# k's maxima by GpSimd in six batches, and the two halves of k'v taken apart, in a kernel that interleaves attention with a feed-forward layer

## The chip, the cores and the metric

The kernel runs on one core of one Trainium2 chip. The metric is the time of one execution on the device in microseconds (us), as the median of several runs. Beside the runs there is one profiled execution, whose trace holds every instruction of every engine. The engines are named as the profile names them: PE (TensorE matmul), PEld (TensorE weight load), DVE (VectorE), ACT (ScalarE), POOL (GpSimd) and SP (SyncE, which here issues nearly all DMAs).

## What is computed

The inputs are q, k and v of 8 batches, 8 heads, 576 rows and 64 columns, and two weights of 512 x 2048 and 2048 x 512. First comes a linear attention, then a feed-forward layer over its 4608 x 512 output:

```python
q_s = exp(q - q.max(-1));  q_s = q_s / (q_s.sum(-1) + 1e-9)      # over the 64 columns
k_s = exp(k - k.max(2));   k_s = k_s / (k_s.sum(2) + 1e-9)       # over the 576 rows
kv  = einsum('bhsd,bhse->bhde', k_s, v)
x   = einsum('bhsd,bhde->bhse', q_s, kv)      # then to rows (batch, row) and columns (head, d)
h   = x @ w_in
out = (h * erf(softplus(h))) @ w_out
```

The maximum of k runs over the rows of a batch, and these lie over the 128 partitions. So it is a maximum over partitions, for each of the 8 x 64 = 512 columns.

## The kernel before

**Feed-forward.** The 4608 rows of x are cut into four pairs of batches, each pair into three blocks of 384 rows, and each block meets four groups of 512 hidden columns: 48 items, n = 0 to 47. For item n the first product runs in four steps `mm1(n, 0..3)`. It is a 2 x 2 block product by seven half-size products: seven calls of `prod` (line 990) of 12 f16 matmuls each, of which `mm1` 0, 1, 2 and 3 hold 2, 2, 1 and 2. DVE and ACT take the results out of three PSUM banks, X, Y and Z. ACT computes softplus and erf, DVE multiplies and splits the result into two f16 halves (`gmul`, `ghi`, `glo`), and `mm2(n, 0..2)` does the second product, 12 f16 matmuls of 512 columns a step (line 1125). The loop from line 1224 writes for each n: `mm1(n, 0)`, `mm2(n-2, 0)`, `mm1(n, 1)`, `mm2(n-2, 1)`, `mm1(n, 2)`, `mm2(n-2, 2)`, `mm1(n, 3)`.

**Attention.** Batch 0 stands in an order written out by hand (line 33), and so does the interleaving of batch 1. Batches 2 to 7 are steps of the generator `attention16` (line 649). At each `yield` it returns a share, a number that stands for how much of the pair's attention this step is. After each `mm2` step the function `pace` (line 1207) takes further steps until the sum of shares has reached a goal that grows with n, a fixed amount for a pair of batches. So there are three slots in each n, here written n.0, n.1 and n.2, at which attention work is put among the feed-forward work. A yield of 0 ends the slot.

A batch goes like this before the change. `k_max` (DVE) takes the maximum of each partition over its rows. `k_max_T` (line 504) transposes the 128 x 512 result with four TensorE transposes into a PSUM bank kT, and a DVE reduce (line 512) gives the column maxima km. `k_max_rows` (line 517) spreads them over all partitions with four more transposes into a PSUM bank kB. DVE subtracts kB from k in three pieces (lines 662 and 667; kt is the batch's 64 last rows) and each row's maximum from q (`q_sub`). ACT takes the exponentials. Then for each of the two halves of four heads: `kv_mm` multiplies k' by v, where a column of ones beside v gives the sums, and `kv_norm` divides; `q_norm` divides q; `q_halves` splits q into two f16 parts (ACT line 640, DVE line 641) and transposes them with a DMA from SP (line 643). After both halves `kv_max` and `kv_split` scale kv into f16 halves in `kvbd` (lines 595, 596), with one more transpose for the scale (`x_bk`, line 125). Last come the products x = q' kv: `xt` for the last rows of the pair, in odd batches only, and four blocks x0 to x3 (line 632).

**What sets the order.** The code's order is not the engines' order. A planner of the framework orders each engine's instructions by when it reckons them ready, so that DVE often works ahead of the code. `tc.issue_after(i)` queues an instruction behind i on its engine. ACT's exponentials, softplus and erf are chained in this way, in the order of the code (`act`, line 339). Each engine runs its queue in order, and so does each DMA queue. v has one buffer for both halves of the heads (`vbuf`), so `load_half(v, "v", b, 1)` waits for the first half's `kv_mm`, and the second half's `kv_mm` waits for that load.

The tiles that the steps below touch: the small SBUF tag `qT` of two buffers (k's maxima, kvf), and two PSUM banks of the tag `bk` (kT, kB, k'v, x_bk, xt, x).

Of the kernel before, what the change touches and what calls it, by code (L numbers as in the profile page):

```python
# [1 line left out]

# [7 lines left out]
F32 = mybir.dt.float32  # L10
# [35 lines left out]
OUTS = [0, 1, 2, 3]  # L46

SHARES = [2.51, 0, 0.16, 0.09, 1.58, 2.43, 1.12, 0.26, 0.29, 0.04, 0.78, 1.12, 0.16]
SHARES16 = [2.51, 0, 0.16, 0.09, 1.58, 2.43, 1.3, 2.43, 1.3, 0.26, 0.3, 0.78, 0.3]
LEAD = 2.0  # L50

EXPMASK = 0x7F800000
# [5 lines left out]
def attn_moe_kernel(  # L58
# [9 lines left out]
    nc = tc.nc  # L68
# [270 lines left out]
    def act(out_, in_, func, chain=True, **kw):  # L339

        with ExitStack() as es:
            if chain and last[0] is not None:
                es.enter_context(tc.issue_after(last[0]))
            i = nc.scalar.activation(out_, in_, func, **kw)  # L344
        if chain:
            last[0] = i.ins
        return i
# [144 lines left out]
    def k_max(b, ks, kt):  # L492

        kmax = at.tile([P, H, D], F32, tag="qT", name=f"kmax_{b}")
        k2 = at.tile([P, 2, 4, D], F32, tag="qT", name=f"k2_{b}")
        for hf in range(2):
            nc.vector.tensor_tensor(k2, ks[hf][:, 0:2], ks[hf][:, 2:4], op=ALU.max)
            nc.vector.tensor_tensor(
                kmax[:, hf * 4:hf * 4 + 4, :], k2[:, 0], k2[:, 1], op=ALU.max
            )  # L500
        nc.vector.tensor_tensor(kmax[kt[1]], kmax[kt[1]], kt[0], op=ALU.max)
        return kmax

    def k_max_T(b, kmax):
        bk = bank(f"kT_{b}")
        km2 = hd(kmax)
        for c in range(NC4):
            nc.tensor.transpose(
                bk[:, c * P:(c + 1) * P], km2[:, c * P:(c + 1) * P], ident
            )  # L510
        km = at.tile([P, NC4], F32, tag="km", bufs=1, name=f"km_{b}")
        nc.vector.tensor_reduce(
            km, bk.rearrange("p (c s) -> p c s", c=NC4), axis=AX.X, op=ALU.max
        )
        return km

    def k_max_rows(b, km):

        bk = bank(f"kB_{b}")
        for c in range(NC4):  # L520
            nc.tensor.transpose(
                bk[:, c * P:(c + 1) * P], km[:, c:c + 1].to_broadcast([P, P]), ident
            )
        return bk.rearrange("p (h d) -> p h d", h=H)

    W = D + 1

    def kv_mm(b, hf):
# [104 lines left out]
                out_, kvbd[b % 2][:, wl, c, :], qT[:, ql], start=(i == 0), stop=(i == 2)  # L633
            )

    def q_halves(src, place, name):

        n = src.shape[1]
        st_ = place.bitcast(F16).rearrange("p (i n) -> p i n", i=2)
        nc.scalar.copy(st_[:, 0], src)  # L640
        nc.vector.tensor_tensor(st_[:, 1], src, st_[:, 0], op=ALU.subtract)
        qT = src.bitcast(F16).rearrange("p (a s) -> p a s", s=P)
        nc.sync.dma_start_transpose(qT, place.bitcast(F16))
        return qT.rearrange("p (i a) s -> p i a s", i=2)

    def flat3(t):
        return t.rearrange("p a b c -> p (a b c)")

    def attention16(b):
        d, j, p = bat[b], b % 2, b // 2  # L650
        even = bat[b - j]
        tl = slice(j * TAIL, (j + 1) * TAIL)
        ks, qs, kt = d["k"], d["q"], even["kt"][tl]
        sh = iter(SHARES16)
        kmax = k_max(b, ks, (kt, tl))
        yield next(sh)
        km = k_max_T(b, kmax)
        q_sub(rows(qs[0]), 16, f"q_{b}_0")
        yield next(sh)
        kb = k_max_rows(b, km)  # L660
        for hf in range(2):
            nc.vector.tensor_tensor(
                ks[hf], ks[hf],
                kb[:, None, hf * 4:hf * 4 + 4, :].to_broadcast([P, TM, 4, D]),
                op=ALU.subtract,
            )
        nc.vector.tensor_tensor(kt, kt, kb[tl], op=ALU.subtract)
        yield next(sh)
        q_sub(rows(qs[1]), 16, f"q_{b}_1")
        if j == 1:  # L670
            q_sub(even["qt"], H, f"qt_{p}")
        yield next(sh)
        for t in (*ks, kt, qs[0], qs[1], *([even["qt"]] if j == 1 else [])):
            act(t, t, AF.Exp, chain=b > 1)
        yield next(sh)
        qT = {}
        for hf in range(2):
            kv_norm(b, hf, kv_mm(b, hf))
            if hf == 0:
                d["v"].append(load_half(v, "v", b, 1))  # L680
            q_norm(rows(qs[hf]), 16, f"q_{b}_{hf}", b)
            yield next(sh)
            qT[hf] = q_halves(flat3(qs[hf]), flat3(ks[hf]), f"{b}_{hf}")
            yield next(sh)
        if j == 1:
            q_norm(even["qt"], H, f"qt_{p}", b)
            qT[2] = q_halves(hd(even["qt"]), hd(even["kt"]), f"{p}_t")
        if b + 1 < B:
            load_kv(b + 1)
        mx = kv_max(b)  # L690
        yield next(sh)
        kv_split(b, mx)
        yield next(sh)
        for i in ((3 * p + 1, 3 * p + 2) if j else (3 * p, 3 * p + 1)):
            while not x_free(i):
                yield 0
        w = next(sh)
        if j == 1:
            bk = bank(f"xt_{p}")
            x = xblock(p * NBK + 1)  # L700
            bk3 = bk.rearrange("p (c s) -> p c s", c=NC4)
            for a in range(2):
                for c in range(NC4):
                    cs = slice(a * TAIL, (a + 1) * TAIL)
                    x_mm(2 * p + a, c, bk3[:, c, cs], qT[2][:, :, c, cs])
            x_put(bk3, x[:, :, SM - T:SM - T + P], None)
            if b + 1 < B:
                bat[b + 1]["qt"] = load_tail(q, "qt", p + 1)
            yield w
        w = next(sh)  # L710
        for c in range(NC4):
            hf, c2 = divmod(c, 2)
            bk = bank(f"x_{b}_{c}")
            q4 = qT[hf].rearrange("p i (t c) s -> p i t c s", c=2)[:, :, :, c2]
            x_mm(b, c, bk.rearrange("p (t s) -> p t s", t=TM), q4)
            x_split(b, c, bk)
            if c2 == 1 and b + 1 < B:
                load_q(b + 1, hf)
            if c == NC4 - 1:
                d["xdone"] = True  # L720
            yield w

    def x_split(b, c, bk, part=None):
        for blk, off, o, w in xcols(b, 0 if b % 2 == 0 else SM + 2 * TAIL, SM)[part or slice(9)]:
# [250 lines left out]
    def mm1(n, k):  # L975

        p, bk, g = seq[n]
        s = st[n]  # L980
        assert ("in", g) in wready
        x = x7[p * NBK + bk]
        jn = wjobs.index(("in", g))
        Th = T // 2
        if k == 0:
            s["H"] = ch.tile([P, FG, T], F32, tag="H", bufs=3, name=f"H_{n}")
        C = {(i, j): s["H"][:, 2 * i:2 * i + 2, Th * j:Th * j + Th]
             for i in range(2) for j in range(2)}

        def prod(b, wi, xi):  # L990
            new = b not in s
            if new:
                s[b] = psh.tile([P, 512], F32, tag=f"p{b}", name=f"p{b}_{n}")
            w = [wop(jn, h, wi, 1)[:, 0] for h in range(2)]
            for a in range(2):
                o = s[b][:, a * Th:(a + 1) * Th]
                for c in range(2):
                    for i, (wl, xl) in enumerate(((0, 0), (0, 1), (1, 0))):
                        nc.tensor.matmul(  # L999
                            o, w[wl][:, c, a * P:(a + 1) * P], x[:, xl, xi, c, :],  # L1000
                            start=(new and a == 0 and c == 0 and i == 0),
                            stop=(c == 1 and i == 2), skip_group_check=True,
                        )

        def bank2(b):
            return s[b][:, :T].rearrange("p (a t) -> p a t", a=2)

        add = nc.vector.tensor_tensor
        if k == 0:
            prod("Y", 1, 1)  # L1010
            nc.vector.tensor_copy(C[0, 0], bank2("Y"))  # L1011
            prod("X", 0, 0)
            add(C[0, 0], bank2("X"), C[0, 0], op=ALU.add)  # L1013
        elif k == 1:
            prod("Z", 6, 3)
            nc.scalar.copy(C[1, 1], bank2("Z"))
            prod("X", 3, 6)
            nc.scalar.copy(C[0, 1], bank2("X"))  # L1018
        elif k == 2:
            prod("X", 5, 5)  # L1020
            add(C[1, 1], bank2("X"), C[1, 1], op=ALU.add)
        else:
            prod("Z", 4, 2)
            add(C[0, 1], bank2("Z"), C[0, 1], op=ALU.add)  # L1024
            prod("X", 2, 4)
            nc.scalar.copy(C[1, 0], bank2("X"))  # L1026

# [173 lines left out]
                assert tok("A"), i  # L1201

    w_odd = sum(SHARES[:11]) + NC4 * sum(SHARES[11:])
    per_pair = 2 * (sum(SHARES16[:11]) + NC4 * SHARES16[12]) + SHARES16[11]
    n1 = NG + 4

    def pace(at_n):
# [68 lines left out]
```

## Time and profile before

| what | value |
|---|---|
| median of 3 runs | 853.0 us (851.73 to 853.64) |
| the profiled execution's own time | 853.86 us |
| its span (first to last instruction in the trace) | 851.7 us |
| busy: PE, PEld, DVE, ACT, POOL | 811.2, 553.8, 638.2, 503.0, 17.6 us |
| mean granted TensorE clock | 0.988 |

A group's row gives line, engine, operation, written tile <- read tiles, shapes and count, then the busy time in us and the mean of one in ns, then the idle time of the engine just before these instructions and what ended it. A row of the timeline gives start and duration in us, engine, line, operation, tiles and count, and in brackets the idle time before it. A row of the waits gives who waited for what: us in total, how many times, the longest. A row of the windows gives the stretch and its length, then each engine's busy time with its count of instructions, the granted clock and the DMA share.

### The profile page before, as it was taken

What the parts mean: (1) busy time and instruction counts of PE and PEld (TensorE: products, weight loads), DVE (VectorE), ACT (ScalarE), POOL (GpSimd) and SP (SyncE); (2) the same over time, 40 slices, a digit from 0 to 9 for tenths busy, and PEclk for the clock granted to TensorE, in tenths of its full rate; (3) what the DMA queues carried; (4) which work ended last, traced back from release to release, by engine and by line L of the source; (5) the groups of instructions that cost most, each with busy time, mean ns of one, the idle gap of its engine ahead of it and who ended that gap; (6) DMA issues with size and microseconds to landing.
All of it is one profiled execution on the core that took longest, in us unless ns stands there. A gap on an engine that the chain in (4) does not pass through costs nothing.

```text
span 851.7 us, 15370 instructions
## 1 busy us (share of the span) xinstructions
PE 811.2 (95%) x6448; PEld 553.8 (65%) x6448; DVE 638.2 (75%) x913; ACT 503.0 (59%) x633; POOL 17.6 (2%) x37
## 2 busy tenths in 40 slices
PE   2999998899999999999999999999999999999997
PEld 1655557567667667766776676766776676777673
DVE  5999899998997879758865779748866657554543
ACT  2598486777564556555673566555663565543532
POOL 2010000000000000000000000000000000000000
PEclk8899999899999999999999999999999999999999
DMA  9997420016416402412134302322121000100100
GB/s 255 407 250 197 120 75 13 1 25 112 106 35 131 108 9 61 103 31 51 51 70 98 87 14 51 93 51 51 38 51 38 38 2 1 38 1 1 38 1 37
DMA packets 145508, 62.59 MB, mean 73 GB/s; under 512 B 134688, under 2 KB 136736, under 8 KB 145440
## 3 DMA queue, kind: packets, MB, share of 16 engines
q1 hardware_dynamic: 143264, 53.23, 25.1%
q0 software_dynamic: 2176, 8.39, 2.8%
q8 instruction: 50, 0.82, 0.4%
q14 instruction: 18, 0.15, 0.1%
HBM read 45.09 MB, written 9.44 MB: 64 GB/s over the span
## 4 chain that ended last, share of the span: by engine, by line
PE 64%; DVE 19%; ACT 10%; issue 3%; SPq 2%; DMA 1%; ACTq 0%; POOL 0%; DVEq 0%
PE o L1125 27%; PE pX L999 15%; PE pZ L999 7%; ACT G L344 4%; PE o L1116 4%; ACT L344 3%; PE pY L999 3%; DVE G L1079 3%; PE kv L542 2%; DVE H L1097 2%; PE pX L1038 2%; DVE H L1093 2%; SPq L409 2%; PE x L632 1%; DVE wi L298 1%
## 5 line engine op out<-in xcount | busy, mean ns | idle before, releaser
L1125 PE MATMUL o<-wo,H 128*128 128x512 f16 x1584 | 367.0, 380 | 2.8 <-DVE H L1093 1.8
L999 PEld LDWEIGHTS <-wi 128*128 128x128 f16 x3696 | 311.2, 98 | 44.3 <-issue 15.7
L1125 PEld LDWEIGHTS <-H 128*128 128x128 f16 x1584 | 152.7, 98 | 157.4 <-DVE H L1093 2.6
L999 PE MATMUL pX<-x,wi 128*128 128x192 f16 x2112 | 206.2, 248 | 7.6 <-ACT H L1018 4.5
L344 ACT ACT_TABLE_LOAD x104 | 133.4, 1283 | 2.8 <-DVE H L1024 0.8
L1079 DVE SCALAR_TENSOR_TENSOR G<-G,small,H 128x1536 f32<-128x1536 f32 x44 | 79.9, 1817 | 56.2 <-ACT G L344 56.0
L1026 ACT COPY H<-pX 128x384 f32<-128x384 f32 x44 | 20.9, 475 | 165.3 <-PE pX L999 159.9
L999 PE MATMUL pZ<-x,wi 128*128 128x192 f16 x1056 | 104.0, 247 | 3.4 <-ACT x L297 1.8
L344 ACT ACTIVATE G<-H,U 128x768 f32<-128x768 f32 (+1 forms) x60 | 72.7, 1231 | 22.1 <-DVE H L1024 21.5
L1097 DVE TENSOR_TENSOR H<-G,H 128x1536 f16<-128x1536 f32 x44 | 77.2, 1755 | 1.0
L344 ACT ACTIVATE G<-G 128x1536 f32<-128x1536 f32 x48 | 71.2, 1484 | 0.5
L999 PE MATMUL pY<-x,wi 128*128 128x192 f16 x528 | 51.9, 247 | 0.0
L1024 DVE TENSOR_TENSOR H<-pZ,H 128x384 f32<-128x384 f32 x44 | 24.4, 554 | 32.5 <-PE pZ L999 32.1
L1011 DVE COPY H<-pY 128x384 f32<-128x384 f32 x44 | 24.3, 553 | 30.3 <-PE pY L999 30.3
L1116 PE MATMUL o<-wo,G 128*128 128x512 f32 x96 | 43.4, 597 | 0.0
L1093 DVE CAST H<-G 128x1536 f16<-128x1536 f32 x44 | 42.1, 957 | 0.8
L297 ACT ACTIVATE x<-x 128x768 f16<-128x768 f32 (+1 forms) x44 | 32.9, 763 | 12.8 <-DVE x L388 11.1
L1141 DVE TENSOR_SCALAR ob<-o,V 128x512 f32<-128x512 f32 x29 | 21.7, 748 | 24.5 <-PE o L1125 24.5
L298 DVE SCALAR_TENSOR_TENSOR x<-x,x 128x768 f16<-128x768 f32 (+1 forms) x44 | 37.0, 851 | 3.2 <-ACT x L297 3.2
L1013 DVE TENSOR_TENSOR H<-pX,H 128x384 f32<-128x384 f32 x44 | 24.4, 554 | 15.9 <-PE pX L999 15.7
L443 ACT ACTIVATE x<-x 128x384 f32<-128x384 f32 (+1 forms) x52 | 17.5, 394 | 30.0 <-PE x L632 27.4
L1116 PEld LDWEIGHTS o<-wo,G 128*128 128x128 f32 x96 | 17.5, 190 | 18.7 <-issue 18.2
(184 smaller groups left out, 762.7 us busy)
## 6 DMA issues: line engine op xcount, KB each, us to landing
out_dram<-ob SPq DMA_DIRECT2D x32, 256.0 KB, 2.4
vbuf<-in_v_dram SPq DMA_DIRECT2D x60, 128.0 KB, 3.1
q<-in_q_dram SPq DMA_DIRECT2D x56, 128.0 KB, 3.4
k<-in_k_dram SPq DMA_DIRECT2D x56, 128.0 KB, 3.1
wo<-in_moe_w_in_dram SPq DMA_DIRECT2D x4, 1024.0 KB, 17.2
wi<-in_moe_w_out_dram POOLq DMA_DIRECT2D x2, 1024.0 KB, 8.9
wi<-in_moe_w_in_dram SPq DMA_DIRECT2D x2, 1024.0 KB, 9.4
raw<-in_moe_w_out_dram POOLq DMA_DIRECT2D x2, 1024.0 KB, 8.0
```

The lines of the kernel that those rows point to most:

```text
L297: nc.scalar.activation(hi, src, AF.Copy, scale=s)
L298: nc.vector.scalar_tensor_tensor(lo, src, s, hi, op0=ALU.mult, op1=ALU.subtract)
L344: i = nc.scalar.activation(out_, in_, func, **kw)
L999: nc.tensor.matmul(o, w[wl][:, c, a * P:(a + 1) * P], x[:, xl, xi, c, :], start=(new and a == 0 and c == 0 and i == 0), stop=(c == 1 and i ...
L1011: nc.vector.tensor_copy(C[0, 0], bank2("Y"))
L1013: add(C[0, 0], bank2("X"), C[0, 0], op=ALU.add)
L1024: add(C[0, 1], bank2("Z"), C[0, 1], op=ALU.add)
L1079: nc.vector.scalar_tensor_tensor(flat(s["G"]), flat(s["G"]), (GB if n in OUT32 else GA)[:, g:g + 1], flat(s["H"]), op0=ALU.mult, op1=ALU.mult,
L1093: nc.vector.tensor_copy(flat(s["gh"]), flat(s["G"]))
L1097: nc.vector.tensor_tensor(flat(s["gl"]), flat(s["G"]), flat(s["gh"]), op=ALU.subtract)
L1116: nc.tensor.matmul(o, s["G"][:, a, ts_], w[:, a, :], start=(first_ and a == 0), stop=(last_ and a == FG - 1),)
L1125: nc.tensor.matmul(o, s[gt][:, a, ts_], w[wl][:, a, :], start=(first_ and a == 0 and i == 0), stop=(last_ and a == FG - 1 and i == 2),)
```

## The change

In batches 2 to 7 the two groups of transposes, the reduce between them and the two PSUM banks are left out. GpSimd's `partition_all_reduce` takes kmax and writes the maximum over all 128 partitions to each of them, into an SBUF tile kB. The subtraction of kB is queued behind the latest `add` from bank Z in `mm1(n, 3)` (line 1024). The second half of k'v and the scaling of kv now stand ahead of the second half of q, and the shares are new.

```diff
+    drained = [None]
+    def k_max_all(b, kmax):
+        kb = at.tile([P, DM], F32, tag="qT", name=f"kB_{b}")
+        nc.gpsimd.partition_all_reduce(kb, hd(kmax), P, bass_isa.ReduceOp.max)
+        return kb.rearrange("p (h d) -> p h d", h=H)
...
-        kmax = k_max(b, ks, (kt, tl))
-        yield next(sh)
-        km = k_max_T(b, kmax)
+        kb = k_max_all(b, k_max(b, ks, (kt, tl)))
+        yield 1.8
         q_sub(rows(qs[0]), 16, f"q_{b}_0")
-        yield next(sh)
-        kb = k_max_rows(b, km)
-        for hf in range(2):
-            nc.vector.tensor_tensor(
-                ks[hf], ks[hf],
-                kb[:, None, hf * 4:hf * 4 + 4, :].to_broadcast([P, TM, 4, D]),
-                op=ALU.subtract,
-            )
-        nc.vector.tensor_tensor(kt, kt, kb[tl], op=ALU.subtract)
-        yield next(sh)
+        yield 0.9
         q_sub(rows(qs[1]), 16, f"q_{b}_1")
         if j == 1:
             q_sub(even["qt"], H, f"qt_{p}")
-        yield next(sh)
+        yield 0.9
+        with tc.issue_after(drained[0]):
+            for hf in range(2):
+                nc.vector.tensor_tensor(
+                    ks[hf], ks[hf],
+                    kb[:, None, hf * 4:hf * 4 + 4, :].to_broadcast([P, TM, 4, D]),
+                    op=ALU.subtract,
+                )
+            nc.vector.tensor_tensor(kt, kt, kb[tl], op=ALU.subtract)
+        yield 0.9
         for t in (*ks, kt, qs[0], qs[1], *([even["qt"]] if j == 1 else [])):
             act(t, t, AF.Exp)
-        yield next(sh)
+        yield 1.5
         qT = {}
-        for hf in range(2):
-            kv_norm(b, hf, kv_mm(b, hf))
-            if hf == 0:
-                d["v"].append(load_half(v, "v", b, 1))
+        def q_half(hf):
             q_norm(rows(qs[hf]), 16, f"q_{b}_{hf}", b)
-            yield next(sh)
-            qT[hf] = q_halves(flat3(qs[hf]), flat3(ks[hf]), f"{b}_{hf}")
-            yield next(sh)
+            yield 0.75
+            qT[hf] = q_halves(flat3(qs[hf]), flat3(ks[hf]))
+            yield 0.75
+        kv_norm(b, 0, kv_mm(b, 0))
+        d["v"].append(load_half(v, "v", b, 1))
+        yield 0.4
+        yield from q_half(0)
+        kv_norm(b, 1, kv_mm(b, 1))
+        mx = kv_max(b)
+        yield 0.6
+        kv_split(b, mx)
+        yield 0.4
+        yield from q_half(1)
         if j == 1:
             q_norm(even["qt"], H, f"qt_{p}", b)
-            qT[2] = q_halves(hd(even["qt"]), hd(even["kt"]), f"{p}_t")
+            qT[2] = q_halves(hd(even["qt"]), hd(even["kt"]))
         if b + 1 < B:
             load_kv(b + 1)
-        mx = kv_max(b)
-        yield next(sh)
-        kv_split(b, mx)
-        yield next(sh)
+        yield 0.75 if j == 1 else 0
...
-            add(C[0, 1], bank2("Z"), C[0, 1], op=ALU.add)
+            drained[0] = add(C[0, 1], bank2("Z"), C[0, 1], op=ALU.add).ins
...
-    per_pair = 2 * (sum(SHARES16[:11]) + NC4 * SHARES16[12]) + SHARES16[11]
+    per_pair = 2 * SHARE16 + 0.75 * 2
```

The old shares of a batch are 2.51, 0, 0.16, 0.09, 1.58, then 2.43 and 1.3 for each half, 0.26, 0.3, 0.78 for xt and 0.3 for each of x0 to x3; a pair makes 27.9. In the new order xt and each of x0 to x3 have 0.75, and a pair makes 28.3.

More of the change, by code (lines that the diff above doesn't have):

```diff
@@ L4 @@
 import concourse.tile as tile
+from concourse import bass_isa
 from concourse import mybir
@@ L48 @@
 SHARES = [2.51, 0, 0.16, 0.09, 1.58, 2.43, 1.12, 0.26, 0.29, 0.04, 0.78, 1.12, 0.16]
-SHARES16 = [2.51, 0, 0.16, 0.09, 1.58, 2.43, 1.3, 2.43, 1.3, 0.26, 0.3, 0.78, 0.3]
+SHARE16 = 1.8 + 0.9 * 3 + 1.5 + 0.4 + 0.75 * 4 + 0.6 + 0.4 + 0.75 * 4
 LEAD = 2.0
@@ L634, in x_mm, with q_halves @@
             )
-    def q_halves(src, place, name):
+    def q_halves(src, place):
         n = src.shape[1]
@@ L653, in attention16 @@
         ks, qs, kt = d["k"], d["q"], even["kt"][tl]
-        sh = iter(SHARES16)
-        kmax = k_max(b, ks, (kt, tl))
-        yield next(sh)
-        km = k_max_T(b, kmax)
+        kb = k_max_all(b, k_max(b, ks, (kt, tl)))
+        yield 1.8
         q_sub(rows(qs[0]), 16, f"q_{b}_0")
-        yield next(sh)
-        kb = k_max_rows(b, km)
-        for hf in range(2):
-            nc.vector.tensor_tensor(
-                ks[hf], ks[hf],
-                kb[:, None, hf * 4:hf * 4 + 4, :].to_broadcast([P, TM, 4, D]),
-                op=ALU.subtract,
-            )
-        nc.vector.tensor_tensor(kt, kt, kb[tl], op=ALU.subtract)
-        yield next(sh)
+        yield 0.9
         q_sub(rows(qs[1]), 16, f"q_{b}_1")
@@ L671, in attention16 @@
             q_sub(even["qt"], H, f"qt_{p}")
-        yield next(sh)
+        yield 0.9
[8 more added lines that the diff above has]
+        yield 0.9
         for t in (*ks, kt, qs[0], qs[1], *([even["qt"]] if j == 1 else [])):
-            act(t, t, AF.Exp, chain=b > 1)
-        yield next(sh)
+            act(t, t, AF.Exp)
+        yield 1.5
         qT = {}
-        for hf in range(2):
-            kv_norm(b, hf, kv_mm(b, hf))
-            if hf == 0:
-                d["v"].append(load_half(v, "v", b, 1))
+        def q_half(hf):
             q_norm(rows(qs[hf]), 16, f"q_{b}_{hf}", b)
-            yield next(sh)
-            qT[hf] = q_halves(flat3(qs[hf]), flat3(ks[hf]), f"{b}_{hf}")
-            yield next(sh)
+            yield 0.75
[11 more added lines that the diff above has]
+        yield from q_half(1)
         if j == 1:
             q_norm(even["qt"], H, f"qt_{p}", b)
-            qT[2] = q_halves(hd(even["qt"]), hd(even["kt"]), f"{p}_t")
+            qT[2] = q_halves(hd(even["qt"]), hd(even["kt"]))
         if b + 1 < B:
             load_kv(b + 1)
-        mx = kv_max(b)
-        yield next(sh)
-        kv_split(b, mx)
-        yield next(sh)
+        yield 0.75 if j == 1 else 0
         for i in ((3 * p + 1, 3 * p + 2) if j else (3 * p, 3 * p + 1)):
@@ L696, in attention16 @@
                 yield 0
-        w = next(sh)
         if j == 1:
@@ L708, in attention16 @@
                 bat[b + 1]["qt"] = load_tail(q, "qt", p + 1)
-            yield w
-        w = next(sh)
+            yield 0.75
         for c in range(NC4):
@@ L720, in attention16 @@
                 d["xdone"] = True
-            yield w
+            yield 0.75
     def x_split(b, c, bk, part=None):
```

## Prediction

> **What bounds the kernel now.** I read the page's busy shares first, then the busy time by stage, then TensorE's waits.
>
> ```profile
> PE 811.2 (95%) x6448; PEld 553.8 (65%) x6448; DVE 638.2 (75%) x913; ACT 503.0 (59%) x633; POOL 17.6 (2%) x37
> ```
>
> ```profile
> 137.00:241.00 104.00, 96.81 (x835) 70.10 (x834) 98.56 (x136) 69.92 (x82) 0.63 (x2) 0.96 0.24 50
> 290.00:484.00 194.00, 190.98 (x1664) 134.66 (x1662) 145.99 (x209) 115.64 (x141) 1.26 (x4) 1.00 0.27 63
> 484.00:678.00 194.00, 191.85 (x1670) 135.30 (x1668) 145.55 (x211) 113.79 (x135) 0.63 (x2) 1.00 0.22 51
> ```
>
> From 290 us on TensorE is busy 190.98 and 191.85 of 194 us at clock 1.00, and DVE 146 of 194: TensorE's own work sets the time. In 137 to 241 us, where batches 2 and 3 begin, DVE (98.56 of 104) is as full as PE (96.81). A busy PE need not be one at its peak, so I look at starts. These rows are PE's queue around the maxima of batch 5.
>
> ```profile
> 401.86 2.75 PE L1125 MATMUL o<-wo,H 128*128 128x512 f16 x12
> 404.45 0.60 PE L508 MATMUL kT<-ident,kmax 128*128 128x128 f32 x4
> 404.89 1.15 PE L999 MATMUL pZ<-x,wi 128*128 128x192 f16 x12
> 405.88 1.15 PE L999 MATMUL pX<-x,wi 128*128 128x192 f16 x12
> ...
> 411.44 0.60 PE L521 MATMUL kB<-ident,km 128*128 128x128 f32 x4
> 411.88 1.15 PE L999 MATMUL pZ<-x,wi 128*128 128x192 f16 x12
> ```
>
> Each group starts where the one before ends: an `mm2` step holds PE 404.45 - 401.86 = 2.59 us, a `prod` 405.88 - 404.89 = 0.99 us. Here a matmul taken away is time gained. The idle PE time that touches this change is small:
>
> ```profile
> PE pX L999 <- ACT H L1018: 4.5, 2, 4.2
> PE xt L632 <- DVE kvbd L595: 2.5, 3, 0.9
> PE x L632 <- DVE kvbd L595: 0.7, 2, 0.4
> PE x L632 <- DVE kvbd L596: 0.6, 3, 0.2
> ```
>
> **The change, part by part.** The sum is made against the profiled execution's own time, 853.86 us; the median shown is 853.0, so 0.9 comes off at the end.
>
> *Transposes taken out.* Four kT transposes hold PE 404.89 - 404.45 = 0.44 us, four kB 411.88 - 411.44 = 0.44 us. Six batches have two groups each: 12 x 0.44 = 5.3 us off a PE that is full. This is the first term.
>
> *The reduce and the subtraction on DVE.*
>
> ```profile
> L512 DVE TENSOR_REDUCE km<-kT 128x4 f32<-128x512 f32 x8 | 5.5, 687 | 6.2 <-PE kT L508 6.2
> L662 DVE TENSOR_TENSOR k<-k,kB 128x1024 f32<-128x1024 f32 x12 | 14.3, 1214 | 0.0
> L455 DVE TENSOR_TENSOR q<-q,q_m 128x1024 f32<-128x1024 f32 x14 | 17.0, 1216 | 0.1
> ```
>
> Six reduces go, 6 x 0.69 = 4.1 us of DVE. The subtraction reads kB from SBUF instead of PSUM: the q subtraction, with both inputs in SBUF, takes 1216 ns against 1214, so nothing changes. I count the 4.1 us at nothing, as DVE has a quarter free in the full PE stretches; in 137 to 241 us it would be worth at most 2 x 0.69 = 1.4 us more.
>
> *The new maximum on POOL.* The trace has no operation over partitions on POOL. Its nearest rows:
>
> ```profile
> L433 POOL MEMSET vtail<- 64x520 f32 x8 | 4.2, 526 | 434.9 <-PE kv L542 355.7 <-issue 79.2
> L871 POOL TENSOR_TENSOR q<-G_raw,q_m 128x1024 f32<-128x1024 f32 x1 | 1.9, 1900 | 13.4 <-DMA v<-in_v_dram 13.4
> ```
>
> One pass over 512 elements with two inputs is 1.90 / 2 = 0.95 us, the low end. Partition after partition, 128 passes at the memset's 0.53 us are 67 us, the high end. A tree over 128 partitions has seven levels: 7 x 0.95 = 6.7 us. I take 6.7, as the row of a real POOL computation is nearer in kind than a serial walk. POOL's queue holds otherwise only the small memsets, so nothing else waits behind it. What waits for it is DVE's in-order queue at the subtraction. The time from the end of k's maxima to that subtraction is the cover:
>
> ```profile
> 223.12 0.69 DVE L501 TENSOR_TENSOR kmax<-kmax,kt 64x512 f32<-64x512 f32 x1
> 240.75 2.35 DVE L662 TENSOR_TENSOR k<-k,kB 128x1024 f32<-128x1024 f32 x2
> ...
> 387.50 0.69 DVE L501 TENSOR_TENSOR kmax<-kmax,kt 64x512 f32<-64x512 f32 x1
> 407.01 0.55 DVE L1024 TENSOR_TENSOR H<-pZ,H 128x384 f32<-128x384 f32 x1
> ```
>
> Batch 3 has 240.75 - 223.81 = 16.9 us. Adding up the new shares against the new goals (28.3 / 24 = 1.18 a slot up to n = 15, 28.3 / 36 = 0.79 after) puts the subtraction into the same slots as before (7.0 and 10.2, then 15.1, 21.0, 27.1, 33.0), now queued behind line 1024, which for batch 5 ended at 407.56: a cover of 407.56 - 388.19 = 19.4 us. So 6.7 us is hidden. Without cover each us would stop DVE, and then PE, six times.
>
> The Trainium skill speaks against this part: its GPSIMD Engine Reference, "Cross-partition — where GPSIMD wins", gives 247,699 ns for a reduce along the partition axis at [128, 2048]; 512 columns would by proportion be an estimated 62 us. No row here shows it. By that page the sum would end near the slow rival's time below.
>
> *The halves in a new order.* kv_split now stands at least two slots ahead of the first product that reads kvbd, where it was in the same or the next one. So the kvbd waits go: 2.5 + 0.7 + 0.6 = 3.8 us, the second term. Every DMA of these steps stays, in a new order on SP: v's second half first, the two q transposes further apart, k's loads for the next batch earlier (3.0 to 4.5 units ahead of its maxima instead of 1.8 to 2.5). Two waits are at risk.
>
> (a) v's second half has fewer slots: 1.9 units from kv0 to kv1 instead of 3.7.
>
> ```profile
> 421.23 0.29 PE L542 MATMUL kv<-vtail,kt 128*64 128x65 f32 x4
> 422.48 2.64 SPq L409 DMA_DIRECT2D vbuf<-in_v_dram  x4
> ...
> vbuf<-in_v_dram SPq DMA_DIRECT2D x60, 128.0 KB, 3.1
> ```
>
> From the last matmul's end (421.52) to the last landing are 0.96 + three issues of 0.66 + 3.1 = 6.0 us. The shares put kv0 of batch 2 in slot 7.2 and kv1 in 8.0, with `mm1` 3 and 0 (four `prod`s) and one `mm2` step between them: 4 x 0.99 + 2.59 = 6.6 us. That covers it by 0.6; all others have two or three slots. I count nothing.
>
> (b) The pair's last q rows are split and transposed late in odd batches. For batch 3 the shares put this and xt in one slot (12.2); for 5 and 7 xt is in the next slot, as it was.
>
> ```profile
> L461 DVE TENSOR_REDUCE qt_r<-qt 128x8 f32<-128x512 f32 x4 | 2.7, 678 | 0.0
> L467 DVE TENSOR_TENSOR qt<-qt,qt_r 128x512 f32<-128x512 f32 x4 | 2.7, 672 | 0.0
> L640 ACT CAST kt<-qt 128x512 f16<-128x512 f32 x3 | 1.9, 626 | 0.0
> L641 DVE TENSOR_TENSOR kt<-qt,kt 128x512 f16<-128x512 f32 x3 | 2.0, 683 | 0.0
> qt<-kt SPq DMA_TRANSPOSE x3, 3.1
> ...
> 473.80 0.51 PE L632 MATMUL xt<-qt,kvbd 128*128 128x64 f16 x12
> ...
> 480.25 0.47 PE L632 MATMUL xt<-qt,kvbd 128*128 128x64 f16 x10
> ```
>
> The chain is 0.68 + 0.67 + 0.63 + 0.68 + 3.1 = 5.8 us and queueing. The last two rows show that the planner spreads xt among other matmuls where its inputs are late, so batch 3 should pay less than 5.8. I add 2.5 us for this and for other waits of the new order; the bounds are 0 and rival B's sum.
>
> **Sum.** 853.86 - 5.3 - 3.8 + 2.5 = 847.3 in a profiled execution, and 846.4 beside the median: 846.5 us. Own range 842 to 851: at the low end no new wait and DVE's 1.4 us, at the high end the transposes' gain with 2 to 3 us of waits beyond the kvbd ones.
>
> **Rivals.**
>
> *B, the new order gives the gain back.* If v's load of batch 2 queues on SP and the late q rows cost their whole chain: 5.8 for batch 3, and 5.8 + 0.6 of queueing less a slot of 2 x 0.99 + 2.59 = 4.6 us, so 1.8, for each of 5 and 7, makes 9.4 against a gain of 9.1. That is 853.0 + 0.3 = 853.3, no change. For it: batch 3's lost slot. Against it: with one slot ahead the list of PE's waits names no transpose. 14%.
>
> *C, POOL holds DVE up.* If DVE can't read two SBUF operands while POOL reads, DVE stands still for each of the six maxima. In 137 to 241 us DVE has 5% free, so two of 6.7 us pass on almost whole (12.7). Later a stop costs what exceeds the 3.6 us of PE work (one `prod` and one `mm2` step) until bank X is wanted again: 4 x 3.1 = 12.4. That is 853.0 - 9.1 + 25 = 869, slower; it eats the gain from about 4 us a maximum on (2 x 3.8 + 4 x 0.4 = 9.2). The trace can't decide it: the DVE subtraction that overlapped POOL's one computation had a single SBUF input, its kB being in PSUM.
>
> ```profile
> 18.12 1.90 POOL L871 TENSOR_TENSOR q<-G_raw,q_m 128x1024 f32<-128x1024 f32 x1 [13.44 <-DMA v<-in_v_dram]
> 17.90 1.20 DVE L859 TENSOR_TENSOR k<-H_raw,kB 128x1024 f32<-128x1024 f32 x1
> ```
>
> Against it: much of DVE's work has no deadline within 6.7 us, as its free quarter shows. The Trainium skill states this lock in SBUF — State Buffer, "SBUF: two separate sides": the pair of ports that DVE and GpSimd share is held for a whole instruction and "the other fully blocks". 13%.
>
> *D, the maximum is a serial walk.* At 67 us against a cover of 19, DVE stops for 48 us in each of six batches, some 4 of them covered by PE's queue: 853 + 6 x 44 = 1117 us. It decides from a maximum of about 21 us on, for batch 3 first. For it: only the missing row. 5%.
>
> *E, the early stall goes too.* The 4.2 us wait of PE for ACT (line 1018) lies in the stretch at clock 0.96; with less DVE work and other slots there it may vanish, and with it the slow clock's share, 0.04 x 104 = 4.2 us: 853.0 - 9.1 - 8.4 = 835.5. Its cause is ACT busy with weight splits, which stay. 6%.
>
> **How the numbers follow.** The forecast has 62%, B 14, C 13, D 5, E 6. 0.2% is 1.7 us, about what this kernel's measurement can tell from no change. Faster: nearly all of the forecast (60), E (6), a little of B (2), 68%. Same: B's middle and the forecast's edge, 14%. Slower: C, D, 18%. The range runs from 840 to 857: out of it are D, most of C and most of E.
>
> **What the profile after would show.** No rows of kT and km for batches 2 to 7, PE's starts closed up by 0.44 us each; no wait of xt or x for kvbd; the POOL maxima below 17 us; no DVE wait for POOL ahead of the subtraction. PE's waits for a transpose or for v would speak for B, lengthened two-input DVE rows during POOL's maxima for C. I am wrong if PE's busy time falls by 5 us and the time doesn't.

## The result, and the profile after

| | median | lowest to highest | ratio to before, 95% interval |
|---|---|---|---|
| before | 853.3 us (4 runs) | 851.7 to 854.3 | |
| after | 865.9 us (4 runs) | 864.0 to 866.7 | 1.0151 [1.0131, 1.0171] |

The change made the kernel 12.6 us slower: 865.9 us, against a forecast of 846.5 and a range of 840 to 857. The span of the profiled execution went from 851.7 to 864.9 us. In the changed kernel a line stands one later than before in the first 520 lines, nine later around `kv_max`, and eleven later in the feed-forward part: 1125 is now 1136, 999 is 1010, 1021 is 1032. In the runs below the numbers differ from these by up to seven.

First the page's busy shares, and the windows that the prediction used, of after. Then the window 343 to 373 us, of after and of before.

```profile
PE 810.5 (94%) x6400; PEld 552.7 (64%) x6400; DVE 639.8 (74%) x907; ACT 502.8 (58%) x633; POOL 34.7 (4%) x43
...
137.00:241.00 104.00, 94.83 (x800) 68.12 (x800) 98.95 (x134) 69.98 (x83) 5.13 (x4) 0.95 0.24 50
290.00:484.00 194.00, 186.72 (x1613) 131.79 (x1611) 145.11 (x208) 109.56 (x131) 8.65 (x6) 0.98 0.27 61
484.00:678.00 194.00, 187.50 (x1613) 131.76 (x1611) 141.05 (x198) 110.97 (x133) 3.89 (x3) 0.98 0.22 51
...
343.00:373.00 30.00, 25.09 (x221) 18.60 (x219) 17.66 (x36) 12.22 (x14) 0.63 (x2) 0.89 0.51 120
```

```profile
343.00:373.00 30.00, 29.47 (x264) 20.72 (x264) 18.90 (x25) 15.11 (x18) 0.63 (x2) 1.00 0.34 84
```

48 matmuls are gone, as planned, but in 290 to 484 us PE is now idle for 7.3 of 194 us where it was 3.0, and the clock has fallen to 0.98. PE's busy time fell by 0.7 us only (811.2 to 810.5), at a lower clock than before. In one window of 30 us PE does 221 matmuls instead of 264. PE's waits of after, the longest first:

```profile
PE kT L509 <- POOL ident masks.py:199: 12.4, 1, 12.4
PE x_bk L126 <- DVE mx L587: 11.8, 5, 5.1
PE pX L1010 <- ACT H L1029: 6.3, 6, 5.0
PE pX L1010 <- DVE H L1032: 4.9, 8, 1.9
...
PE xt L641 <- DVE kvbd L604: 0.3, 1, 0.3
PE xt L641 <- DVE kvbd L605: 0.2, 1, 0.2
```

Two rows are new at the top: the transpose for kv's scale waits for DVE's `mx`, and the very first transposes wait for POOL's identity. The waits for kvbd are nearly gone (0.5 us left of 3.8).

The two long waits for `mx` are in batches 4 and 6. Rows of the timeline of after show batch 4 on DVE, on PE and ACT, and on SP; PE's last two rows are from batch 3, for a comparison below, and from batch 6:

```profile
355.73 0.69 DVE L498 TENSOR_TENSOR k<-k 128x512 f32<-128x512 f32 x1 [5.17 <-DMA k<-in_k_dram]
356.34 1.81 DVE L1090 SCALAR_TENSOR_TENSOR G<-G,small,H 128x1536 f32<-128x1536 f32 x1
...
363.56 0.42 DVE L587 TENSOR_REDUCE mx<-kvf 128x1 f32<-128x256 f32 x1
```

```profile
350.10 1.48 ACT L345 ACTIVATE G<-G 128x1536 f32<-128x1536 f32 x1
...
364.04 0.47 PE L126 MATMUL x_bk<-ident,mx 128*128 128x128 f32 x1 [4.91 <-DVE mx L587]
...
364.73 2.12 PE L1010 MATMUL pZ<-x,wi 128*128 128x192 f16 x12
...
244.31 1.15 PE L1010 MATMUL pX<-x,wi 128*128 128x192 f16 x12 [1.85 <-DVE H L1032]
...
562.73 0.47 PE L126 MATMUL x_bk<-ident,mx 128*128 128x128 f32 x1 [5.08 <-DVE mx L587]
```

```profile
344.56 2.02 SPq L652 DMA_TRANSPOSE q<-k  x1
...
350.60 2.58 SPq L410 DMA_DIRECT2D k<-in_k_dram  x4
```

And the row of SP's waits of after that holds these loads:

```profile
SPq L410 <- DMA q<-k: 20.8, 10, 4.0
```

DVE's row at 355.73 is the first step of `k_max` of the next batch, and it stands ahead of this batch's work in DVE's queue. It waits 5.17 us for k. That k was loaded only from 350.60 on: the tile it goes to is the staging place of the q transpose on SP at 344.56, and SP holds the load until that has landed. Behind it in the same queue are the product G (its erf had ended on ACT at 350.10 + 1.48 = 351.58), its splits, kv's division and `mx`. So PE waits 4.91 us, and after that a group of 12 matmuls takes 2.12 us instead of 1.15, at a lower clock: the window has 0.89, and 0.11 x 30 = 3.3 us. Wait and slow clock make 8.2 us, and batch 6 has the same wait with 5.08 us. The Trainium skill, TensorE: Matmul & The Clock Gate, "Part 1: The HAM clock gate", says that the clock halves after an idle window of about 3.4 us; the trace agrees, as the group behind the wait of 4.91 us takes 2.12 us and the one behind 1.85 us takes 1.15.

GpSimd's maxima in the groups by line, and a row of POOL's start in the timeline, both of after:

```profile
L532 POOL PARTITION_ALL_REDUCE kB<-kmax x6 | 16.9, 2820 | 125.3 <-DVE kmax L502 106.6 <-PE pX L1010 18.7
```

```profile
12.06 0.28 POOL masks.py:199 TENSOR_SCALAR_AFFINE_SELECT ident<-ident 128x128 f32<-128x128 f32 x1 [10.19 <-issue]
```

A maximum takes 2.82 us in the mean (1.78 to 4.12), and the list of DVE's waits of after names none for POOL. At the start POOL now stands 10.19 us ahead of the identity's second step. In the kernel before, the same step and PE's first wait read:

```profile
1.92 0.29 POOL masks.py:199 TENSOR_SCALAR_AFFINE_SELECT ident<-ident 128x128 f32<-128x128 f32 x1
```

```profile
PE kT L508 <- DVE kmax L501: 9.0, 1, 9.0
...
PE pX L999 <- DVE H L1021: 1.5, 3, 0.9
...
PE pX L999 <- ACT H L1026: 1.3, 2, 0.6
```

The last two rows are wanted further down.

### The profile page after: what moved, and what is told of

Its sections match the earlier page's. It is cut to its first block, busy times and chain, and to the rows that moved or that the text cites. A ratio compares the mean times of both kernels' runs of the same rounds, so it can differ in the third digit from the quotient of the medians.

```text
span 864.9 us, 15269 instructions
## 1 busy us (share of the span) xinstructions
PE 810.5 (94%) x6400; PEld 552.7 (64%) x6400; DVE 639.8 (74%) x907; ACT 502.8 (58%) x633; POOL 34.7 (4%) x43
## 4 chain that ended last, share of the span: by engine, by line
PE 55%; DVE 22%; ACT 11%; issue 4%; DMA 4%; SPq 1%; ACTq 0%; DVEq 0%
PE o L1136 22%; PE pX L1010 13%; PE pZ L1010 6%; ACT G L345 4%; ACT L345 4%; PE o L1127 3%; DVE G L1090 3%; PE pY L1010 3%; DVE H L1108 2%; DVE x L299 2%; PE pX L1049 2%; DVE wi L299 2%; PE x L641 2%; DMA q<-in_q_dram 1%; PE kv L551 1%
## 5 line engine op out<-in xcount | busy, mean ns | idle before, releaser
L1010 PEld LDWEIGHTS <-wi 128*128 128x128 f16 x3696 | 314.7, 99 | 52.0 <-issue 23.1
L1024 DVE TENSOR_TENSOR H<-pX,H 128x384 f32<-128x384 f32 x44 | 24.4, 554 | 13.9 <-PE pX L1010 13.6
```

The lines of the kernel that those rows point to most:

```text
L1010: nc.tensor.matmul(o, w[wl][:, c, a * P:(a + 1) * P], x[:, xl, xi, c, :], start=(new and a == 0 and c == 0 and i == 0), stop=(c == 1 and i ...
```

## The experiments

A table of the trace shows where the time came in: the start of the first second-product matmul of item n, less that of the kernel before, in us. All kernels of the table are explained below.

```
n                            4      15      16      27      28      47
after                     +2.17   +2.50  +10.30   +7.45  +15.07  +13.25
held maxima (e1)          +1.64   +0.80   +1.54   -1.17   -0.42   -2.20
GpSimd's maxima (e3)      +4.34   +5.50   +5.50   +9.86   +9.86  +12.93
new order alone (e4)      -1.91   -0.10   +1.83   -0.91   +1.08   -0.81
e3 with subtraction held  +1.54   +1.49   +1.48   +0.77   +0.77   +1.52
```

**1. The next batch's maxima held behind this batch's kv maximum.** My theory: the row at 355.73 is the cause, by its place in DVE's queue. `kvm[0]` is the reduce in `kv_max`.

```diff
+        kvm[0] = nc.vector.tensor_reduce(
...
-        kb = k_max_all(b, k_max(b, ks, (kt, tl)))
+        with tc.issue_after(kvm[0]):
+            kmax = k_max(b, ks, (kt, tl))
+        kb = k_max_all(b, kmax)
```

> The kernel after, with the first maximum of the next batch's k queued on DVE behind this batch's kv maximum; seven DVE instructions change places, nothing else of DVE's or ACT's order. Theory (a wait for a DMA at the head of DVE's queue): the 4.9 and 5.1 us waits of PE for the kv maximum of batches 4 and 6 go, and with them the 6.8 us of half clock behind each (3.4 us lost each) and the delayed softplus products: 15 to 16 us off, 849 to 852 us. Rival (the scale's transpose simply stands too early in PE's queue, whoever is ahead on DVE): PE still waits 4 us and more there, 862 to 866 us.

Measured: 852.0 us, ratio 0.9992 [0.9978, 1.0007], against 1.0151: 0.0159, or 13.6 us. Both steps of the table, at n = 16 and 28, are gone. Batch 4 in the timeline of this kernel:

```profile
349.92 1.82 DVE L1094 SCALAR_TENSOR_TENSOR G<-G,small,H 128x1536 f32<-128x1536 f32 x1 [1.07 <-ACT G L345]
...
357.48 0.68 DVE L498 TENSOR_TENSOR k<-k 128x512 f32<-128x512 f32 x1
...
357.62 0.32 PE L126 MATMUL x_bk<-ident,mx 128*128 128x128 f32 x1 [0.42 <-DVE mx L589]
```

G goes at 349.92 instead of 356.34, the maximum finds its k loaded, and PE waits 0.42 us. Beside these maxima the hold moves hardly anything (one drain of bank Z on DVE and two of the scale's transposes on PE, by one or two places). So nearly the whole loss of the change is one place in a queue, in two batches. But the 9.1 us of gain that I had forecast do not come out either.

**2. Each of GpSimd's maxima three times.** This tells whether GpSimd holds DVE up.

```diff
         nc.gpsimd.partition_all_reduce(kb, hd(kmax), P, bass_isa.ReduceOp.max)
+        for _ in range(2):
+            nc.gpsimd.partition_all_reduce(kb, hd(kmax), P, bass_isa.ReduceOp.max)
```

> The kernel after with each of POOL's six maxima done three times in a row (the same result written again), all other queues in the same order. Rival (POOL holds DVE's second port, or is late): twelve more maxima of 1.8 to 4.1 us lengthen DVE's two-input instructions and the time by 10 us and more, 875 to 890 us. Theory (POOL gives way and is hidden by a cover of 9 us or more): under 2 us more, 865 to 868 us; DVE's busy time rises by less than 5 us.

Measured: 867.7 us, ratio 1.0176 [1.0142, 1.0210]; 12 more maxima make 1.8 us, not resolved from nothing. GpSimd beside DVE isn't the cause. There is an effect on single instructions: beside the longest maximum of after (471.56 to 475.68 in its timeline) DVE's conversion of G took 1.68 us, where the fourth kernel below, without GpSimd's maxima, has 0.96 for the same item. Two rows of after, and then one of the fourth kernel:

```profile
473.34 1.68 DVE L1104 CAST H<-G 128x1536 f16<-128x1536 f32 x1
...
471.56 4.12 POOL L532 PARTITION_ALL_REDUCE kB<-kmax  x1 [16.69 <-DVE kmax L502]
```

```profile
465.59 0.96 DVE L1106 CAST H<-G 128x1536 f16<-128x1536 f32 x1
```

**3 and 4. Each half of the change alone.** The third kernel has GpSimd's maxima in the old order with the old shares, the fourth has the new order with the transposes. The third against before:

```diff
-        kmax = k_max(b, ks, (kt, tl))
+        kb = k_max_all(b, k_max(b, ks, (kt, tl)))
         yield next(sh)
-        km = k_max_T(b, kmax)
...
-        kb = k_max_rows(b, km)
```

The fourth against after:

```diff
-        kb = k_max_all(b, k_max(b, ks, (kt, tl)))
+        kmax = k_max(b, ks, (kt, tl))
         yield 1.8
+        km = k_max_T(b, kmax)
...
         yield 0.9
+        kb = k_max_rows(b, km)
         with tc.issue_after(drained[0]):
```

> The kernel before with the maxima of batches 2 to 7 on POOL and without their transposes, in the old order and shares. Theory (the loss belongs to the order of the halves, the gain of 5.3 us of PE to POOL's part): 847 to 851 us. Rival (POOL's part itself costs, by its library and DVE's port): 855 to 862 us.

> The kernel after with the maxima by transposes as before, in the new order and shares. Theory (the loss belongs to the new order): the waits of PE for the kv maximum in batches 4 and 6 stand, 866 to 873 us, that is the kernel after plus up to 5.3 us of transposes. Rival (the loss needs POOL): no such wait, 850 to 856 us.

Measured: 866.1 us, 1.0150 [1.0126, 1.0174], for the maxima alone, and 854.6 us, 1.0009 [0.9992, 1.0027], for the order alone. Both forecasts of my theory missed: the loss needs GpSimd's maxima, and these alone cost as much as the whole change. In the fourth kernel the same k is late too, but the planner has put the next batch's maximum one place further back, as the timeline of the fourth kernel shows:

```profile
349.03 1.82 DVE L1092 SCALAR_TENSOR_TENSOR G<-G,small,H 128x1536 f32<-128x1536 f32 x1 [1.07 <-ACT G L345]
351.90 0.69 DVE L498 TENSOR_TENSOR k<-k 128x512 f32<-128x512 f32 x1 [1.05 <-DMA k<-in_k_dram]
352.51 0.95 DVE L1106 CAST H<-G 128x1536 f16<-128x1536 f32 x1
```

Behind G it waits 1.05 us, ahead of G 5.17. Not all of that is the place: k came 2.9 us after erf's end here (351.90 less 349.0), and 4.15 in after (355.73 less 351.58).

In the third kernel the 13 us are spread: 4.3 by n = 4 and then 1 to 2 us at several places (n = 20, 25 and 32 among them). The first column is to be read with care, because the start differs from one profiled execution to the next: the first matmul into bank X starts at 29.87, 28.65 and 30.73 us in the three kernels without GpSimd's maxima (before, the fourth, the tenth), and at 32.94 in the third against 31.22 in the seventh, whose code is the same up to there. So some 2 us of a row can be scatter of the start. PE's waits of the third kernel name the drains of the first product:

```profile
PE kT L509 <- POOL ident masks.py:199: 12.9, 1, 12.9
PE pX L1004 <- ACT H L1023: 10.4, 8, 5.0
PE pX L1004 <- DVE H L1026: 9.0, 9, 2.0
```

Before the change it was 1.5 us for that DVE drain (line 1021 then). So two more causes are to be told apart: the start, and what the drains wait for.

**5 and 6. GpSimd's first program brought back.** I read the 10.19 us of POOL at the start as a change of program: the maxima need another than the identity, the kernel ends with that one in place, and the next execution must load the first one again. One small addition on GpSimd behind batch 7's maximum, with nothing else moved, would make that load in the middle of the kernel. The sixth kernel has this and the hold of the first.

```diff
+        if b == B - 1:
+            z = at.tile([P, 1], F32, tag="zz", bufs=1, name="zz")
+            nc.gpsimd.tensor_tensor(z, ident[:, 0:1], kb[:, 0, 0:1], op=ALU.add)
         yield 0.9
```

> After, with one addition on a single column done by GpSimd behind batch 7's maximum, so that its first program is the last one used; the order of the other engines is that of after. Theory (the program left behind by the previous execution makes the start late): GpSimd's identity of the first microseconds no longer waits (10.2 us of idle before it in after, none in before), PE's first wait for a transposed k falls from 12.4 us on the identity to about 9 us on the DVE maximum (8.8 us in the run with the new order and the transposes kept), the first second product of item 4 starts about 3.5 us earlier (156.96 with maxima, 153.40 without), and the time is about 862.5 us. Rival (the late start comes from the order of the loads or from the k of batch 0): the start stays and the time stays at 866 us, or rises by the second change of program near 590 us.

> After with both: the next batch's k maxima behind this batch's kv maximum on DVE, and the addition on GpSimd behind batch 7's maximum. Theory (two separate costs, the late k maximum and the start): the gains add, 852.0 less 3.5 us gives 848.5 us, ratio to before about 0.995, and the removed transposes then show in full. Rival (the start is hidden by batch 0's loads): 852 us, ratio 0.999.

Measured: 862.0 us, 1.0121 [1.0104, 1.0138], with the addition alone, and 849.4 us, 0.9970 [0.9959, 0.9981], with both. POOL's timeline and PE's first wait in the fifth kernel:

```profile
2.15 0.29 POOL masks.py:199 TENSOR_SCALAR_AFFINE_SELECT ident<-ident 128x128 f32<-128x128 f32 x1 [0.29 <-POOL kvbd L108]
...
584.21 0.18 POOL L681 TENSOR_TENSOR zz<-ident,kB 128x1 f32<-128x1 f32 x1 [7.68 <-issue]
```

```profile
PE kT L509 <- DVE kmax L502: 8.9, 1, 8.9
```

The identity is there at 2.15 us again, PE's first wait is 8.9 us on DVE as before the change, and the load now stands as 7.68 us of idle ahead of the addition at 584.21, where nothing waits for it. The late start cost 0.0030 in one pair of kernels and 0.0022 in the other, and 0.0039 in a third pair, the seventh and ninth kernels below: 1.9 to 3.3 us, less than the 3.5 expected. The sixth kernel's expected ratio of 0.995, with the removed transposes in full, was not reached; it lies outside the interval. The Trainium skill, GPSIMD Engine Reference, "2.1 Instruction dispatch", gives about 6 us for the first call of a freshly loaded program; here it was 10.2 and 7.7 us. That the load falls into the next execution's start fits all profiles: the identity's second step comes at 12.0 to 12.7 us in the six kernels that end with the maxima, and at 2.15 us in the three with the addition.

**7 and 8. The subtraction held, or not.** In the new order the change holds the subtraction of the maximum behind a drain of the first product. The seventh kernel is the third with this hold, put in as below; the eighth takes the same line out of the first experiment.

```diff
+        with tc.issue_after(drained[0]):
             for hf in range(2):
                 nc.vector.tensor_tensor(
```

> Old order and shares with GpSimd's maxima in place of the transposes (866.1 us without more), and the subtraction of the maximum from k held on DVE behind the sum of an MLP product out of pZ, as the changed kernel holds it. Theory (without PE's transposes ahead of it the subtraction goes early and pushes the drains of pX behind other DVE work; the 9.0 us of PE waits for the DVE drain at the pX addition are its price): those waits fall to 2 or 3 us and the time to about 857 to 860 us, which still holds the late start. Rival (the loss is in what GpSimd does beside DVE, or in the start alone): the time stays at 864 to 867 us.

> After with the next batch's k maxima behind this batch's kv maximum on DVE, but without the hold on the subtraction. Theory (a subtraction free to go early costs about 1.5 us per batch by late drains of pX): 852.0 plus 6 to 9 us, 858 to 861 us. Rival (in the new order the place of the subtraction doesn't matter): 852 us.

Measured: 855.3 us, 1.0036 [1.0021, 1.0050], with the hold in the old order, against 1.0150 without; and 857.0 us, 1.0065 [1.0047, 1.0084], without it in the new order, against 0.9992 with. So a subtraction free to move costs 0.0114 or 9.7 us in the old order and 0.0073 or 6.2 us in the new one. The timeline of the third kernel in batch 5, and then the same drain in that of the kernel before:

```profile
395.67 2.36 DVE L667 TENSOR_TENSOR k<-k,kB 128x1024 f32<-128x1024 f32 x2 [1.99 <-POOL kB L530]
...
410.64 1.75 DVE L1102 TENSOR_TENSOR H<-G,H 128x1536 f16<-128x1536 f32 x1
412.31 0.56 DVE L1026 TENSOR_TENSOR H<-pX,H 128x384 f32<-128x384 f32 x1
...
412.92 1.15 PE L1004 MATMUL pX<-x,wi 128*128 128x192 f16 x12 [1.81 <-DVE H L1026]
```

```profile
403.40 0.55 DVE L1021 TENSOR_TENSOR H<-pX,H 128x384 f32<-128x384 f32 x1
403.87 1.75 DVE L1097 TENSOR_TENSOR H<-G,H 128x1536 f16<-128x1536 f32 x1
...
412.31 1.21 DVE L662 TENSOR_TENSOR k<-k,kB 128x1024 f32<-128x1024 f32 x1
```

Before the change the subtraction came 8.9 us behind this drain, as it had to wait for PE's transposes. Without them DVE has it some 17 us ahead of the drain, where it even waits 1.99 us for GpSimd, and the feed-forward work of DVE runs later: the drain now stands behind the split product (line 1102, 1097 before), where it stood ahead of it. PE waits 1.81 us for it. In the seventh kernel the waits for this drain fall from 9.0 to 4.0 us. The transposes had kept DVE's queue in a good order without being meant to.

**9 and 10. Each half of the change at its best.** The ninth kernel is the seventh with the addition on GpSimd; the tenth is the new order with transposes and the hold of the first experiment. Both put together edits shown above.

> Old order and shares, GpSimd's maxima in place of the transposes, the subtraction held, and GpSimd's first program brought back behind batch 7's maximum. Theory (the removed 5.3 us of transposes are real, but in the old order PE spends them on waits for drains of pX: 6.5 us more of those waits with the held subtraction than in the kernel before): the late start goes, 2.6 us less than without the addition, and nothing else: ratio to before 1.000 to 1.001, some 852 to 853 us. Rival (the transposes' 5.3 us come out once the start is mended): ratio 0.994 to 0.996.

> The new order and shares with the transposes kept, and the next batch's k maxima behind this batch's kv maximum on DVE. Theory (with the transposes kept the late k maximum cost little: 4.5 us of PE waits for the kv maximum against 2.6 us with the hold): ratio to before falls from 1.0009 to about 0.999, 2 us less. Then the order alone is worth about nothing and GpSimd's maxima another 0.002. Rival (the held order itself is the gain of the best kernel, whatever makes the maxima): ratio 0.997, the same as with GpSimd's maxima.

Measured: 852.8 us, 0.9997 [0.9982, 1.0012], and 850.9 us, 0.9979 [0.9964, 0.9993]. The late start and the free subtraction mended, GpSimd's maxima in the old order are worth nothing that can be measured. This is so although PE's busy time falls by 5.6 us against before, as the page of the ninth kernel and then its PE waits show:

```profile
PE 805.6 (95%) x6400; PEld 547.4 (64%) x6400; DVE 636.8 (75%) x907; ACT 503.3 (59%) x633; POOL 30.9 (4%) x44
```

```profile
PE pX L1010 <- ACT H L1029: 8.3, 8, 5.0
PE pX L1010 <- DVE H L1032: 4.0, 6, 1.7
...
PE pX L1010 <- DVE H L1024: 0.7, 1, 0.7
...
PE pX L1010 <- ACT H L1037: 0.4, 1, 0.4
```

PE waits 13.4 us for drains of bank X (8.3 + 4.0 + 0.7 + 0.4); before the change it was 7.3 (4.5 + 1.5 + 1.3). The 6.1 us more are about the transposes' 5.3. By the timeline of the ninth kernel, 5.6 us of them begin at a place where transposes were taken out or within 9 us behind it; two of the longest are:

```profile
239.83 1.15 PE L1010 MATMUL pX<-x,wi 128*128 128x192 f16 x12 [1.72 <-DVE H L1032]
...
611.84 1.15 PE L1010 MATMUL pX<-x,wi 128*128 128x192 f16 x12 [1.27 <-ACT H L1029]
```

So PE comes earlier and waits. This is read from one profile of each kernel; no run kept the transposes and held the subtraction in the old order, so a cost of the hold itself isn't ruled out.

The new order alone gives 0.0021; with GpSimd's maxima 0.0030. These two intervals overlap, so whether the maxima add anything to the new order stays open. At most it is an estimated 0.0027 or 2.3 us (0.0009, and the two half widths added as squares), under half of 5.3. The sixth kernel, 849.4 us, has the lowest ratio of all.

## Why the prediction was wrong

**"Transposes taken out", 5.3 us.** The matmuls went, but the rule behind the term, "a matmul taken away is time gained", failed. The ninth kernel shows it with the disturbances taken out: PE's work fell by 5.6 us and the time by a share of 0.0003. PE's queue was full there, but the drains of bank X, ACT's as well as DVE's, came only just in time; PE came earlier and waited. The term was worth 0 in the old order, and in the new one at most 2.3 us.

**The reduce at nothing, the maximum on POOL.** Neither shows a cost of its own in these runs, apart from the change of program below. I had 6.7 us a maximum and it was 2.82; the cover of 16.9 to 19.4 us was far more than needed. The Trainium skill's 247,699 ns at four times the columns (GPSIMD Engine Reference, "Cross-partition — where GPSIMD wins") is not what this instruction takes.

**"The kvbd waits go", 3.8 us.** They went: 3.8 to 0.5. In time the new order gave 0.0021, 1.8 us, and only once the next batch's maximum was held: `kv_max` now stands close ahead of a PE transpose that waits for it, and before the change no such wait was listed. The sixth kernel's waits still have:

```profile
PE x_bk L126 <- DVE mx L589: 2.6, 5, 0.8
```

**"Two waits are at risk."** The failing step. Of the two, neither was the one: the list of PE's waits of after names neither a load of v nor a transpose of q, so (a) and (b) cost nothing there. (With the transposes kept, PE's waits of the fourth and tenth kernels do name (b), once for 1.9 us.) What decided was a third, PE's wait for `mx` behind the next batch's `k_max`, 4.91 and 5.08 us long: I had read k's loads as safer because they came earlier against the maxima's place in the code, and did not ask where the planner would put those maxima in DVE's queue, nor that k's load waits for the q transpose out of the same tile. I named what is queued behind the subtraction and not what is queued behind `k_max`. "I add 2.5 us" stood for 13.6 us in two places, and its upper bound, rival B's sum of 9.4, was too low too.

**What was not in the prediction at all.** The program change on GpSimd at the start of each execution, 1.9 to 3.3 us. And why the transposes stood in the way usefully: with them gone the subtraction could go early, which the change itself keeps from happening by its hold, and which costs 6.2 us where the hold is taken out.

**The rivals.** C (the shared port) came out nearest in time, 869 to 866, for a reason that these runs speak against: a DVE row beside a maximum grew by 0.7 us, but twelve more maxima cost 1.8 us by the medians, where C has 25 for six. B had the right kind of end, a new wait in the new order, at the wrong place. D is out with 2.82 us. E's early stall did not go; it grew from 4.2 to 5.0 us. My own test, "I am wrong if PE's busy time falls by 5 us and the time doesn't", was met by the ninth kernel.

Open is why the planner puts the next batch's maximum ahead of G with GpSimd's maxima and behind it with the transposes; its estimates were not looked at. Open is also whether the held subtraction costs something of its own in the old order.

## What to carry over

When an operation leaves one engine, ask what it kept in order on the others: an in-order queue filled by a planner is shuffled by every removed dependence, and one instruction that waits for a DMA at the head of a queue costs all that stands behind it. Look for every buffer that has two uses, and follow its next load back to the release. A full PE queue does not mean that a matmul taken away is gained: look how late the drains come that the next matmuls need, because they decide once PE comes earlier.

## What was not expected of the hardware

A maximum over all 128 partitions of 512 f32 columns on GpSimd takes 1.78 to 4.12 us. By the fifth, sixth and ninth kernels it needs a program of its own: the way back to the first one takes 6.9 to 7.7 us of POOL in the middle of a kernel and 10.1 to 10.8 at its start, and a kernel that ends with the other program pays this at its next start. A PE idle time of 5 us costs some 3 us more, as the groups behind it take 2.12 us instead of 1.15.
